# An attention-and-mixer kernel on one core: attention's work items given new spacings, the turned queries scaled in two instructions, and more filler matmuls in the first batch

## The chip, the core and the metric

The kernel runs on one core of one Trainium2 chip. The metric is device time in microseconds (us), lower is better. A single execution was also taken by the hardware profiler; the trace comes from that execution. The engines are named as in the profile: PE (TensorE, matmuls; PEld are its weight loads), DVE (VectorE), ACT (ScalarE), POOL (GpSimd) and SP (SyncE, which here only issues DMAs; SPq is its queue). L402 is line 402 of the kernel before.

## The reference, cut to what matters

```
q, k, v: 8 batches x 12 heads x 448 tokens x 64        (float32)
q_n = q / sqrt(mean(q*q) + 1e-6) * g_q                  (k_n likewise with g_k)
attn = softmax(q_n @ k_n^T / 8) @ v                     per head
x = attn as 8 x 448 x 768                               heads side by side
u = x + ((x^T @ U) @ V)^T                               rank 32, over the tokens
out = u + relu(u @ w_ch1) @ w_ch2                       768 -> 3072 -> 768
```

So each of the 8 batches has an attention part (12 heads) and a mixer part (the rank-32 step and the two large matmuls). The two large matmuls are most of PE's work.

## The kernel before, in words

**Units.** Heads are handled in pairs, six pairs to a batch; two pairs (four heads) form a group, so there are 24 groups, 0 to 23, three to a batch. A group's q, k and v are loaded together by `load`.

**Preparing a group.** `squares` (L138 on ACT or L140 on POOL) squares q and k, `sums` (L159, DVE) adds up each token's squares, `roots` (L165 and L166, ACT) makes the reciprocal root, and `scale` or `scale_dma` (POOL: L169, or L188 and L192) multiplies q and k with it, giving `qn` and `kp`. `values` (L196, L198) casts v. `scale_all` is roots, both scalings and values. Then q and k must be turned so that the 64 features lie on partitions. Groups 0 to 5 (batches 0 and 1) are turned by PE: `turn` (L343, seven transposes of 128 columns), followed by copies on DVE (`take_q` L352, which also multiplies by the gain `gg`; `take_k` L358 and L361). Groups 6 to 23 are turned by DMA: `turn_dma` issues four DMA transposes on SP, in the order q of the first pair (L367), k of the first pair (L369), q of the second, k of the second. Then `take_dma` multiplies the turned q by the gain, on POOL (L374), in one instruction over both pairs. It writes in place, so the scores of either pair read its result.

**Attention of a pair (b, pr).** The scores lie with keys on partitions, in four row blocks r = 0 to 3. `Sc` (L402) is the matmul of one block; r = 0, 1, 2 are two matmuls of 64 rows each (one for each head, on the two halves of the array), r = 3 is one matmul of 128 rows for the last 64 keys of both heads. The exponential of the block follows on ACT (L403) and writes `E`. The score tiles of r < 3 take turns in two PSUM buffers (`ps_sc`); all other PSUM tiles share four (`ps`). `V` (L420, L424) is one half of attn @ v, for 256 queries. It needs the exponentials of all four blocks. Its result is divided by the row sums on DVE (L427, L428) into x.

**The mixer of a batch.** `mix_t` and `mix_tr` (L441, L448) are the rank-32 step's first half, `mix_rows` (L490, L493) its second; DVE adds x (L498), and the sum is turned by a DMA transpose on SP (L502) into `uT`. In batch 0 `mix`, `mix_t0` and `up_part` do the same with PE. `up(b, ht)` (L508) is one of 24 blocks of the first large matmul, six matmuls of 448 columns; relu on ACT (L510). `down` (L534) is a quarter of one output tile of the second large matmul, six matmuls of 384 columns; DVE adds u (L542) and SP stores (L550).

**What sets the order.** All engines run their own queue in the order in which the program emits instructions. The emission is one list on the attention side (`att`) and one on the mixer side (`mlp`). Each item has a cost, given by hand. After the first batch's attention, the loop at L765 takes the next attention item as soon as the attention cost so far (`ca`) is not above `due(cm)`, the share that corresponds to the mixer cost emitted so far (`cm`), and otherwise a mixer item. So a larger cost on an attention item means that more of the mixer is emitted *behind* it before the next attention item. Items of cost 0 (loads, scalings, sums) follow at once. Attention runs ahead of the mixer by 1.8 batches (`LEAD`).

**The order on the attention side** for batches 1 to 7 is written in the loop at L613. For the first pair of a group (a = 0): the scores r = 0 and 1; V of the pair before, both halves; then three score blocks in one item (r = 2 of this pair, r = 0 of the next pair, r = 3 of this pair), so three exponentials come in a row; the group after is scaled (`scale_all`) or turned (`turn_dma`, `take_dma`); the first half of V. For the second pair (a = 1): r = 1, 2, 3 in one item; for groups up to 5 the two turns `T`; the second half of V of the pair before.

**The first batch** has no mixer work to put beside attention. Its items are listed in `extra` (L578), with `keep_busy(n)` (L232) after some score blocks: n matmuls of 128 columns of the identity by itself, which nobody reads.

Of the kernel before, what the change touches and what calls it, by code (L numbers as in the profile page):

```python
# [13 lines left out]
ALU = AluOpType  # L14
# [10 lines left out]
def kernel(  # L25
# [13 lines left out]
    nc = tc.nc  # L39
# [213 lines left out]
    gg = consts.tile([P, 2], FP32)  # L253
# [117 lines left out]

    def take_dma(gi):
        qT = q_bufs[gi % 2]
        nc.gpsimd.tensor_scalar(qT, qT, gg[:, 0:1], None, ALU.mult)  # L374
        for a in range(2):
            qk[(gi, a)] = [qT[:, a], kT_bufs[gi % 2][:, a]]

    def T(gi, i):
        if gi >= DMA_FROM:
            if i == 0:  # L380
                take_dma(gi)
            return
        turn(gi, i)
        for a in range(2):
            (take_q, take_k)[i](gi, a)
# [167 lines left out]
    pairs = [(b, pr) for b in range(B) for pr in range(NPAIR)]  # L553
    att = []

    def add_att(cost, f, *a):
        att.append((cost, f, a))
# [9 lines left out]
    def V2(i, half):  # L567
        return (0.55, V, (*pairs[i], half))
# [3 lines left out]
    def scales(gi):  # L572
        return [(0, roots, (gi,)), (0, scale, (gi, 0, pool)), (0, scale, (gi, 1, pool))]

    def turns(gi):
        return [(0.4, turn, (gi, 0)), (0, take_q, (gi, 0)), (0, take_q, (gi, 1)), (0.4, turn, (gi, 1)), (0, take_k, (gi, 0))]
# [3 lines left out]
        (0, 1): [(0, keep_busy, (8,))],  # L580
        (0, 2): scales(1) + [(0, squares, (2, 1, pool)), (0, keep_busy, (8,))],
        (0, 3): [(0, keep_busy, (8,))],
        (1, 1): [V2(0, 0)],
        (1, 2): [(0.4, turn, (1, 0)), (0, take_q, (1, 0)), (0, take_q, (1, 1))],
        (1, 3): [(0.4, turn, (1, 1)), (0, take_k, (1, 0)), V2(0, 1), (0, take_k, (1, 1)), (0, sums, (2, 1)),
                 (0, values, (1,)), (0, load, (4,)), (0, weights, (1,))],
        (2, 1): scales(2) + [(0, weights, (1,)), V2(1, 0)],
        (2, 3): [V2(1, 1), (0, prep_u, ())],
        (3, 1): [V2(2, 0)],
        (3, 2): turns(2),  # L590
        (3, 3): [V2(2, 1), (0, take_k, (2, 1)), (0, squares, (3, 0, pool)), (0, values, (2,)), (0, load, (5,)),
# [21 lines left out]
    for i, (b, pr) in enumerate(pairs):  # L613
        if b == 0:
            continue
        gi, a = divmod(i, 2)
        more = gi + 1 < len(groups)
        by_dma = gi + 1 >= DMA_FROM
        soon = gi + 2 < len(groups)

        nxt = pairs[i + 1 - a]

        if pr == 0 and b > 1:
            add_att(0.55, V, *pairs[i - 1], 0)
            add_att(0.55, V, *pairs[i - 1], 1)
        if a == 0:
            add_att(0.5, Srows, ((b, pr, 0), (b, pr, 1)))
            if i == 2 * DMA_FROM - 2:
                add_att(0.0, load, DMA_FROM + 1)
            if by_dma and more:  # L630
                add_att(0.0, scale_all, gi + 1)
            if b == 1 and pr == 0:
                add_att(0.4, lambda: None)
            if not by_dma:
                add_att(0.0, squares, gi + 1, 0, nc.gpsimd)
                add_att(0.0, squares, gi + 1, 1, nc.gpsimd)
                if gi + 2 >= DMA_FROM:
                    add_att(0.0, load, gi + 2)
            if pr != 0:
                add_att(0.55, V, *pairs[i - 1], 0)  # L640
                add_att(0.55, V, *pairs[i - 1], 1)
            add_att(0.7, Srows, ((b, pr, 2), (*nxt, 0), (b, pr, 3)))
            if not by_dma:
                add_att(0.0, sums, gi + 1, 0)
                add_att(0.0, sums, gi + 1, 1)
            if more and by_dma:
                add_att(0.0, turn_dma, gi + 1)
                add_att(0.0, take_dma, gi + 1)
                if gi + 1 == DMA_FROM:
                    add_att(0.0, weights, 2)  # L650
                if gi + 3 < len(groups):
                    add_att(0.0, load, gi + 3)
            if not by_dma:
                add_att(0.0, scale_all, gi + 1)
            add_att(0.55, V, b, pr, 0)
        else:
            add_att(0.7, Srows, ((b, pr, 1), (b, pr, 2), (b, pr, 3)))
            if more and not by_dma:
                add_att(0.39, T, gi + 1, 0)
            if soon and gi + 2 >= DMA_FROM:  # L660
                add_att(0.0, squares, gi + 2, 0)
                add_att(0.0, squares, gi + 2, 1)
            add_att(0.55, V, *pairs[i - 1], 1)
            if more and not by_dma:
                add_att(0.39, T, gi + 1, 1)
            if soon and gi + 2 >= DMA_FROM:
                add_att(0.0, sums, gi + 2, 0)
                add_att(0.0, sums, gi + 2, 1)
# [96 lines left out]
    while ia < len(att) or im < len(mlp):  # L765
# [6 lines left out]
        if take_att:  # L772
            c, f, a = att[ia]
# [11 lines left out]
        else:  # L785
            c, f, a, _ = mlp[im]
# [34 lines left out]
```

## Time and profile before

| what | us |
|---|---|
| median of three timed runs (597.79 to 599.4) | 598.76 |
| the profiled execution's own time | 596.07 |
| its span in the profile | 594.3 |
| PE busy in it | 574.3 |
| ACT busy | 307.4 |
| POOL busy | 201.9 |
| DVE busy | 196.5 |

The profiled execution's own time is 1.8 us more than its span, which begins and ends with the first and last recorded instruction. In the profile's timeline a row gives the start of the first and the length until the modelled end of the last of a run of like instructions, and in brackets how long the engine had been idle before and what ended that. Matmuls overlap: a run of six `up` matmuls has a length of 1.30 us, but the next instruction starts 1.13 to 1.14 us after it. So an idle time in brackets is a little shorter than the time by which the next matmul was late.

### The profile page before, as it was taken

What the parts mean: (1) busy time and instruction counts of PE and PEld (TensorE: products, weight loads), DVE (VectorE), ACT (ScalarE), POOL (GpSimd) and SP (SyncE); (2) the same over time, 40 slices, a digit from 0 to 9 for tenths busy, and PEclk for the clock granted to TensorE, in tenths of its full rate; (3) what the DMA queues carried; (4) which work ended last, traced back from release to release, by engine and by line L of the source; (5) the groups of instructions that cost most, each with busy time, mean ns of one, the idle gap of its engine ahead of it and who ended that gap; (6) DMA issues with size and microseconds to landing.
All of it is one profiled execution on the core that took longest, in us unless ns stands there. A gap on an engine that the chain in (4) does not pass through costs nothing.

```text
span 594.3 us, 11608 instructions
## 1 busy us (share of the span) xinstructions
PE 574.3 (97%) x4792; PEld 333.5 (56%) x4792; DVE 196.5 (33%) x454; ACT 307.4 (52%) x482; POOL 201.9 (34%) x288
## 2 busy tenths in 40 slices
PE   8799998999999999999999999999999999999996
PEld 7554455555566555655566555565556655655563
DVE  6775544512334312621235320541234310410011
ACT  7767784467453775466753568346753254014200
POOL 6995565243153333515053514424243000000000
PEclk9899999999999999999999999999999999999999
DMA  9999999573346550693164742566015210220022
GB/s 233 200 241 239 257 193 195 118 191 72 101 90 173 146 127 16 120 238 100 36 150 99 180 106 34 147 152 175 2 34 112 50 28 0 60 68 1 0 55 53
DMA packets 104508, 68.19 MB, mean 115 GB/s; under 512 B 66568, under 2 KB 101256, under 8 KB 104456
## 3 DMA queue, kind: packets, MB, share of 16 engines
q1 hardware_dynamic: 95044, 58.03, 41.0%
q0 software_dynamic: 9408, 9.44, 9.6%
q8 instruction: 37, 0.61, 0.4%
q14 instruction: 15, 0.12, 0.1%
q10 hardware_dynamic: 4, 0.00, 0.0%
HBM read 52.20 MB, written 11.01 MB: 106 GB/s over the span
## 4 chain that ended last, share of the span: by engine, by line
PE 90%; DMA 3%; ACT 3%; POOL 1%; DVE 1%; SPq 1%; issue 1%; POOLq 0%; ACTq 0%
PE ph L508 36%; PE po L534 36%; PE pv L424 6%; PE sc L402 5%; ACT E L403 2%; PE sl L402 2%; PE pv L420 2%; PE pm L493 2%; DMA qT<-qn 1%; DMA vf<-in_v_dram 1%; POOL qT L374 1%; PE pt L343 1%; PE pu L441 1%; DVE ssq L159 1%; ACT hT L510 0%
## 5 line engine op out<-in xcount | busy, mean ns | idle before, releaser
L534 PE MATMUL po<-w2b,hT 128*128 128x384 bf16 x1344 | 238.0, 326 | 0.0
L508 PE MATMUL ph<-uT,w1b 128*128 128x448 bf16 x1140 | 229.4, 352 | 0.0
L403 ACT ACTIVATE E<-sc,gg 128x896 bf16<-128x896 f32 (+1 forms) x150 | 140.3, 990 | 120.6 <-PE sc L402 120.4
L534 PEld LDWEIGHTS <-hT 128*128 128x128 bf16 x1344 | 126.0, 98 | 77.3 <-issue 3.7
L510 ACT ACTIVATE hT<-ph 128x448 bf16<-128x448 f32 x190 | 102.1, 548 | 119.7 <-PE ph L508 118.7
L508 PEld LDWEIGHTS <-w1b 128*128 128x128 bf16 x1140 | 108.0, 98 | 95.2 <-issue 3.0
L188 POOL TENSOR_TENSOR qn<-qf,rs 128x384 bf16<-128x384 f32 x36 | 29.9, 829 | 140.5 <-ACT rs L166 137.4
L427 DVE RECIPROCAL r<-pv 128x4 f32<-128x4 f32 x96 | 17.5, 182 | 178.9 <-PE pv L424 178.5
L374 POOL TENSOR_SCALAR qT<-qT,gg 128x896 bf16<-128x896 bf16 x18 | 45.4, 2522 | 90.1 <-DMA qT<-qn 68.9
L542 DVE TENSOR_TENSOR ob<-po,x 128x384 f32<-128x384 f32 x48 | 26.7, 557 | 115.4 <-PE po L534 115.4
L424 PE MATMUL pv<-va,E 128*128 128x65 bf16 x1152 | 57.6, 194 | 0.0
L424 PEld LDWEIGHTS <-E 128*128 128x128 bf16 x1152 | 51.0, 98 | 6.3 <-issue 0.2
L402 PE MATMUL sc<-qT,kT 64*128 64x448 bf16 (+1 forms) x294 | 43.9, 356 | 7.9 <-ACT E L403 3.8
L159 DVE TENSOR_REDUCE ssq<-sq 128x14 f32<-128x896 f32 x45 | 46.7, 1077 | 3.2 <-ACT sq L138 3.1
L420 PE MATMUL pv<-vl,E 128*128 128x130 bf16 x192 | 42.4, 221 | 2.8 <-ACT E L403 2.7
L428 DVE TENSOR_TENSOR x<-pv,r 128x256 bf16<-128x256 f32 x96 | 40.8, 425 | 3.3
L402 PEld LDWEIGHTS <-kT 64*128 64x128 bf16 (+1 forms) x336 | 14.1, 94 | 46.1 <-issue 42.6
L498 DVE TENSOR_TENSOR x<-pm,x 128x384 bf16<-128x384 f32 x48 | 26.5, 554 | 23.4 <-PE pm L493 19.3
L188 POOL TENSOR_TENSOR kp<-kf,rs 128x384 bf16<-128x384 f32 x36 | 29.8, 828 | 0.0
L403 ACT ACTIVATE E<-sl,gg 128x448 bf16<-128x448 f32 x42 | 26.9, 639 | 0.0
L420 PEld LDWEIGHTS <-E 128*128 128x128 bf16 x192 | 18.8, 98 | 13.1 <-ACT E L403 5.0
L196 POOL CAST va<-vf 128x768 bf16<-128x768 f32 x24 | 20.6, 860 | 0.0
(92 smaller groups left out, 299.7 us busy)
## 6 DMA issues: line engine op xcount, KB each, us to landing
qf<-in_q_dram SPq DMA_DIRECT2D x23, 448.0 KB, 3.6
kf<-in_k_dram SPq DMA_DIRECT2D x23, 448.0 KB, 5.6
out_dram<-ob SPq DMA_DIRECT2D x50, 192.0 KB, 2.7
vf<-in_v_dram SPq DMA_DIRECT2D x48, 192.0 KB, 5.9
w1b<-in_moe_w_ch_dram POOLq DMA_DIRECT2D x4, 1152.0 KB, 18.2
w2b<-in_moe_w_ch_dram POOLq DMA_DIRECT2D x8, 576.0 KB, 14.0
vf<-in_v_dram SPq DMA_DIRECT2D x48, 32.0 KB, 4.9
out_dram<-ob SPq DMA_DIRECT2D x12, 96.0 KB, 3.4
```

The source lines that it names most:

```text
L159: nc.vector.tensor_reduce(ssqs[gi][:, i, :], sqs.pop((gi, i)), AX, ALU.add)
L188: nc.gpsimd.tensor_tensor(main.rearrange("p (t i) d -> p i t d", i=2), src[:, c, :2 * NJ].rearrange("p (i t) d -> p i t d", i=2), rs[:, c, ...
L374: nc.gpsimd.tensor_scalar(qT, qT, gg[:, 0:1], None, ALU.mult)
L402: nc.tensor.matmul(sc[:, i, :S], kT[d, keys], qT[d], start=True, stop=True)
L403: nc.scalar.activation(es[(b, pr)][:, 2 * r:2 * r + n, :], sc[:, :n, :S], AF.Exp, scale=scal, bias=bias)
L420: nc.tensor.matmul(pv[:, i].rearrange("p e d -> p (e d)"), E[:, 2 * NJ, w:w + P], vl[:, lp, :], start=True, stop=False)
L424: nc.tensor.matmul(pv[:, i, e, :], E[:, 2 * j + e, w:w + P], va[:, (first_h + step * e) * NJ + j, :], start=False, stop=(e == 1 and j == N ...
L428: nc.vector.tensor_tensor(xs[b].rearrange("p i (h d) -> p i h d", d=D)[:, 2 * half:2 * half + 2, h0:h0 + step + 1:step, :], pv[:, :, :, :D ...
L508: nc.tensor.matmul(ph, w1b[:, dt, ht * P:(ht + 1) * P], uT[:, dt, off:off + S], start=(dt == 0), stop=(dt == KD - 1))
L510: nc.scalar.activation(hT[:, ht, off:off + S], ph, AF.Relu)
L534: nc.tensor.matmul(po, hT[:, ht, col:col + P], w2b[:, ht, half * HALF:(half + 1) * HALF], start=(ht == 0), stop=(ht == KH - 1))
L542: nc.vector.tensor_tensor(ob[:, h], po, urows(b, col, half), ALU.add)
```

## The change

Three things are changed.

1. `take_dma` scales the turned q pair by pair: two POOL instructions of 448 columns in place of one of 896.
2. Five `keep_busy` items are added to the first batch: 8 matmuls after the scores (1, 0), 6 after V in (1, 1), 8 after the turn in (1, 2), 6 after (2, 2) and 6 after (3, 0); with the existing fillers of 8 in (0, 0) to (0, 3) there are nine.
3. The costs in the loop are changed: 0.5 to 0.45 for the pair of score blocks, 0.7 to 1.0 for the three score blocks of a first pair, 0.7 to 0.6 for those of a second pair, 0.55 to 0.4 or 0.5 for the halves of V, 0.4 to 0.8 for an empty item at the start of batch 1. Both turns `T` of a group now follow each other on the list, ahead of the second half of V. The rest of the list is in the same order as before: the V items of a batch's first pair are only written at another place, and `(b, pr + 1, 0)` is what `(*nxt, 0)` was.

```diff
     def take_dma(gi):
         qT = q_bufs[gi % 2]
-        nc.gpsimd.tensor_scalar(qT, qT, gg[:, 0:1], None, ALU.mult)
         for a in range(2):
+            nc.gpsimd.tensor_scalar(qT[:, a], qT[:, a], gg[:, 0:1], None, ALU.mult)
             qk[(gi, a)] = [qT[:, a], kT_bufs[gi % 2][:, a]]
...
-        (1, 1): [V2(0, 0)],
-        (1, 2): [(0.4, turn, (1, 0)), (0, take_q, (1, 0)), (0, take_q, (1, 1))],
+        (1, 0): [(0, keep_busy, (8,))],
+        (1, 1): [V2(0, 0), (0, keep_busy, (6,))],
+        (1, 2): [(0.4, turn, (1, 0)), (0, take_q, (1, 0)), (0, take_q, (1, 1)), (0, keep_busy, (8,))],
...
+        (2, 2): [(0, keep_busy, (6,))],
         (2, 3): [V2(1, 1), (0, prep_u, ())],
+        (3, 0): [(0, keep_busy, (6,))],
...
-        if pr == 0 and b > 1:
-            add_att(0.55, V, *pairs[i - 1], 0)
-            add_att(0.55, V, *pairs[i - 1], 1)
         if a == 0:
-            add_att(0.5, Srows, ((b, pr, 0), (b, pr, 1)))
+            if pr == 0 and b > 1:
+                add_att(0.5, V, *pairs[i - 1], 0)
+                add_att(0.5, V, *pairs[i - 1], 1)
+            add_att(0.45, Srows, ((b, pr, 0), (b, pr, 1)))
...
             if b == 1 and pr == 0:
-                add_att(0.4, lambda: None)
+                add_att(0.8, lambda: None)
...
             if pr != 0:
-                add_att(0.55, V, *pairs[i - 1], 0)
-                add_att(0.55, V, *pairs[i - 1], 1)
-            add_att(0.7, Srows, ((b, pr, 2), (*nxt, 0), (b, pr, 3)))
+                add_att(0.4, V, *pairs[i - 1], 0)
+                add_att(0.5, V, *pairs[i - 1], 1)
+            add_att(1.0, Srows, ((b, pr, 2), (b, pr + 1, 0), (b, pr, 3)))
...
-            add_att(0.55, V, b, pr, 0)
+            add_att(0.4, V, b, pr, 0)
         else:
-            add_att(0.7, Srows, ((b, pr, 1), (b, pr, 2), (b, pr, 3)))
+            add_att(0.6, Srows, ((b, pr, 1), (b, pr, 2), (b, pr, 3)))
             if more and not by_dma:
                 add_att(0.39, T, gi + 1, 0)
+                add_att(0.39, T, gi + 1, 1)
...
-            add_att(0.55, V, *pairs[i - 1], 1)
-            if more and not by_dma:
-                add_att(0.39, T, gi + 1, 1)
+            add_att(0.5, V, *pairs[i - 1], 1)
```

More of the change, by code (lines that the diff above doesn't have):

```diff
@@ L619 @@
         soon = gi + 2 < len(groups)
-        nxt = pairs[i + 1 - a]
-        if pr == 0 and b > 1:
-            add_att(0.55, V, *pairs[i - 1], 0)
-            add_att(0.55, V, *pairs[i - 1], 1)
         if a == 0:
-            add_att(0.5, Srows, ((b, pr, 0), (b, pr, 1)))
+            if pr == 0 and b > 1:
+                add_att(0.5, V, *pairs[i - 1], 0)
+                add_att(0.5, V, *pairs[i - 1], 1)
+            add_att(0.45, Srows, ((b, pr, 0), (b, pr, 1)))
             if i == 2 * DMA_FROM - 2:
```

## The prediction

> **What bounds the kernel now.** I read the page first, then a table of stretches, then PE's timeline where it idles.
>
> ```profile
> span 594.3 us, 11608 instructions
> ...
> PE 574.3 (97%) x4792; PEld 333.5 (56%) x4792; DVE 196.5 (33%) x454; ACT 307.4 (52%) x482; POOL 201.9 (34%) x288
> ```
>
> PE works 97% of the span, so a change can only gain what PE idles (20.0 us) or what PE does more slowly than it could. The table says where the idle lies (columns: stretch, length, busy of each engine, granted clock, DMA share, GB/s).
>
> ```profile
> 0.00:45.00 45.00, 37.49 (x460) 27.34 (x461) 31.96 (x89) 32.44 (x50) 37.10 (x53) 0.96 0.98 224
> 45.00:120.00 75.00, 68.20 (x625) 38.95 (x623) 36.02 (x86) 45.70 (x71) 39.43 (x49) 1.00 1.02 203
> 120.00:370.00 250.00, 250.00 (x2072) 141.13 (x2069) 76.74 (x167) 148.65 (x233) 90.79 (x139) 1.00 0.49 115
> 370.00:380.00 10.00, 9.27 (x105) 5.90 (x104) 5.20 (x11) 4.73 (x8) 5.61 (x7) 1.00 0.59 151
> ```
>
> Before 45 us PE idles 7.51 us, from 45 to 120 (batch 1's attention and its mixer neighbours) 6.80, near 375 once 0.73, and nowhere else until the last 5.0 of the 20.0, at the end. So from 120 us on new spacings can only lose; the prize lies before. PE's timeline names every gap of the first of these:
>
> ```profile
> 50.28 0.36 PE L402 MATMUL sc<-qT,kT 64*128 64x448 bf16 x2 [0.41 <-ACT E L403]
> ...
> 50.77 0.33 PE L490 MATMUL pm<-x,Vm 128*128 128x384 bf16 x1
> 50.94 1.30 PE L508 MATMUL ph<-uT,w1b 128*128 128x448 bf16 x6
> 53.03 0.23 PE L420 MATMUL pv<-vl,E 128*128 128x130 bf16 x1 [0.80 <-ACT E L403]
> ...
> 61.06 0.55 PE L402 MATMUL sc<-qT,kT 64*128 64x448 bf16 x4 [0.45 <-DVE kT L358]
> ...
> 66.21 0.55 PE L402 MATMUL sc<-qT,kT 64*128 64x448 bf16 x4
> 66.69 0.36 PE L402 MATMUL sl<-qT,kT 128*128 128x448 bf16 x1
> 66.89 0.33 PE L490 MATMUL pm<-x,Vm 128*128 128x384 bf16 x1
> 67.05 1.30 PE L508 MATMUL ph<-uT,w1b 128*128 128x448 bf16 x6
> 69.23 0.23 PE L420 MATMUL pv<-vl,E 128*128 128x130 bf16 x1 [0.88 <-ACT E L403]
> ...
> 76.41 0.55 PE L402 MATMUL sc<-qT,kT 64*128 64x448 bf16 x4
> ...
> 84.41 0.23 PE L420 MATMUL pv<-vl,E 128*128 128x130 bf16 x1 [1.04 <-ACT E L403]
> ...
> 84.91 1.14 PE L534 MATMUL po<-w2b,hT 128*128 128x384 bf16 x6
> 85.98 0.55 PE L402 MATMUL sc<-qT,kT 64*128 64x448 bf16 x4
> ...
> 91.07 1.14 PE L534 MATMUL po<-w2b,hT 128*128 128x384 bf16 x6
> 94.01 0.56 PE L402 MATMUL sc<-qT,kT 64*128 64x448 bf16 x4 [1.80 <-POOL qT L374]
> ...
> 114.33 0.56 PE L402 MATMUL sc<-qT,kT 64*128 64x448 bf16 x4 [1.42 <-POOL qT L374]
> ```
>
> The seven idles add up to 6.80, the whole of it. A late matmul costs a little more than its idle: the six matmuls at 67.05 are followed after 1.14 when nothing waits, so V at 69.23 could have begun at 68.19 and is 1.04 late. In the same way the seven are late by 0.57, 0.96, 0.51, 1.04, 1.20, 1.87 and 1.50, together 7.65 us.
>
> Two kinds matter. V, at 53.03, 69.23 and 84.41, is emitted too close behind three exponentials; scores, at 94.01 and 114.33, wait for the scaling of the turned q.
>
> **Part 1: spacing behind the three exponentials.** From the first of the three score blocks at 66.21 to V at 69.23 are 3.02 us: that is the time which ACT needs. PE's work between them is blocks 0.68, `mix_rows` 0.16, one `up` 1.14: 1.98. I lay out the changed order with these prices, and with V 0.49 (84.41 to 84.91), `down` 0.97 and 0.10 to enter 64-row scores (84.91 to 85.98 together):
>
> - V of (1, 2): two `up` now lie between, 3.12. The wait of 1.04 goes.
> - V of (1, 4): `up` and `down`, 2.79. 1.20 becomes 0.23.
> - V of (1, 0): still `up` and `mix_rows`, 1.98, so 1.04 remains. But its second score block no longer waits for a score buffer, since two `up` and a `mix_rows` now precede it: 0.57 + 0.96 becomes 1.04.
> - Scores at 61.06: V and an `up` now lie between the turn and them. 0.51 goes.
> - Batches 2 to 7: the shortest such distance was 2.96 and becomes 4.27. PE has no idle there today, so nothing is gained.
>
> What is late next? The turns of groups 4 and 5 on PE, which follow sooner, while their preparation hangs on the same exponentials:
>
> ```profile
> 66.75 1.90 ACT L403 ACTIVATE E<-sc,gg 128x896 bf16<-128x896 f32 x2
> ...
> 69.96 0.32 ACT L165 ACTIVATE rs<-ssq,eps 128x28 f32<-128x28 f32 x1 [0.35 <-DVE ssq L159]
> ```
>
> ```profile
> 54.37 1.69 POOL L169 TENSOR_TENSOR qn<-qf,rs 128x896 bf16<-128x896 f32 x1 [6.24 <-DVE x L428]
> ...
> 70.61 1.69 POOL L169 TENSOR_TENSOR qn<-qf,rs 128x896 bf16<-128x896 f32 x1 [6.53 <-ACT rs L166]
> 72.26 1.69 POOL L169 TENSOR_TENSOR kp<-kf,rs 128x896 bf16<-128x896 f32 x1
> ```
>
> From `mix_rows` (whose DVE addition stands ahead of the sums) to a finished qn are 5.29 us in group 4 (50.77 to 56.06) and 5.41 in group 5 (66.89 to 72.30); roots, scaling and turn queue behind one another. Changed order, counted from the first of the three blocks: in group 4 `mix_rows` comes at 1.82, so qn is ready at about 7.15, while PE reaches the turn at 3.02 + 0.49 + 1.14 + 0.10 + 0.68 + 1.14 = 6.57: a new wait of 0.60. In group 5 `mix_rows` comes at 0.68, and one more relu stands ahead of the roots: qn at 6.2 against PE at 5.53, a new wait of 0.72; then the turn of k, at 7.78 against 7.89, 0.11.
>
> Balance of this part: 0.57 + 0.96 + 0.51 + 1.04 + 1.20 = 4.28 before, 1.04 + 0.60 + 0.72 + 0.11 + 0.23 = 2.70 after, **gain 1.6**.
>
> **Part 2: q scaled per pair.**
>
> ```profile
> 82.13 1.32 SPq L367 DMA_TRANSPOSE qT<-qn  x1
> 84.20 1.20 SPq L369 DMA_TRANSPOSE kT<-kp  x1
> 85.50 1.20 SPq L367 DMA_TRANSPOSE qT<-qn  x1
> ```
>
> ```profile
> 85.47 1.71 POOL L281 DMA_DIRECT2D w2b<-in_moe_w_ch_dram  x2
> 91.43 2.52 POOL L374 TENSOR_SCALAR qT<-qT,gg 128x896 bf16<-128x896 bf16 x1 [4.25 <-DMA qT<-qn]
> ```
>
> ```profile
> 85.50 5.73 DMA qT<-qn
> ```
>
> The one scaling waits for the *second* pair's q (issued 85.50, landed 91.23) though the scores at 94.01 need the first pair's, issued 3.4 us earlier. In the changed program each half waits for its own transpose. Price of a half: between 1.26 (half of 2.52) and 2.52 (all fixed cost); POOL's scaling of 896 columns takes 1.69 (L169) and of 384 columns 0.82, so nearly proportional, and I take 1.26. For the first q's landing no row stands alone: its issue plus 5.73 is 87.86. POOL is free at 87.18, so q is ready at 87.86 + 0.20 + 1.26 = 89.3, 12.9 us after the scores (1, 4, 0), which began at 76.41; k of the same pair is issued earlier than the second q and lands between. The scores wanted both at 92.14. But the order takes 1.1 us of PE work out of that distance, and the wait at 84.41 shrinks: PE asks 13.6 us after (1, 4, 0). Slack 0.7, so **1.87 goes**. With a half at 2.52 a wait of 0.6 would stay. The second pair's scores come 6.4 us later; with the same 5.73 its k (issued 1.25 after q) is there 3.8 us before.
>
> Group 7 (114.33): the first pair's q is issued two transposes (2.5 us) before the second's and its half takes 1.26 less, so it is ready 3.8 earlier. Against that, PE work between `turn_dma` and the scores falls by 1.1 (9.5 to 8.4), and one more x transpose stands ahead on SP, at most 1.3: 1.4 remain, and I count **the 1.50 as gone.** Groups 8 to 23 lose up to 2.3 us of distance and gain the 3.8; today none of them waits.
>
> **Part 3: the fillers.** Thirty-four matmuls.
>
> ```profile
> 11.30 0.62 PE L235 MATMUL busy<-ident 128*128 128x128 bf16 x8
> ```
>
> Eight last 0.62, the modelled tail included, so 34 cost at most 34/8 of it, 2.6 us, if on the path. Their cover is the waiting of PE in the first batch, for ACT and POOL:
>
> ```profile
> PE sc L402 <- ACT E L403: 3.4, 7, 0.9
> ...
> PE pt L343 <- POOL kp L169: 0.9, 1, 0.9
> ```
>
> Each new filler stands ahead of one of these waits or of the turn that waits for POOL, and holds PE for at most 0.62; I cost them at 0 (range 0 to 0.8 if the score behind a filler reaches ACT late). What they may bring is the clock:
>
> ```profile
> 21.69:25.10 3.41, 1.87 (x29) 1.27 (x29) 2.81 (x7) 3.12 (x6) 2.98 (x3) 1.00 0.49 84
> 25.10:28.51 3.41, 3.41 (x37) 2.71 (x34) 3.21 (x8) 2.50 (x4) 3.39 (x3) 0.50 1.11 213
> ```
>
> A stretch with PE busy for 1.87 of 3.41 is followed by one at half clock. The fillers after (2, 2) and (3, 0) put 0.67 into the first. At full clock the second would take PE up to 1.7 less, but DVE is behind it:
>
> ```profile
> 27.97 0.38 DVE L361 COPY kT<-pt 64x64 bf16<-64x64 bf16 x2
> ```
>
> That is the end of kT for the next scores, 28.35; they began 0.36 later, at 28.71. DVE's queue ahead of it (sums, casts, copies) does not depend on PE's clock. So 0.3 is gained, from 0 (the stretch stays slow) to 1.7. The Trainium skill's page "TensorE: Matmul & The Clock Gate", in "Why this matters for your kernels", asks for "No PE-idle gaps >~3µs between matmul bursts" against a fall to half clock. By that rule the fillers would change nothing, as no idle here is that long, and 0.3 would fall out of the sum, which would be 5.0 and 593.8; but this trace does show half clock behind idles of at most 0.89 us, so the row decides.
>
> **Sum.** 1.6 + 1.87 + 1.50 + 0.3 = 5.3 us off the profiled execution's own 596.07 (span 594.3 and 1.8 around it): 590.8. The median of the timed runs is 598.76, 2.7 above the profiled one; I carry the gain over unchanged: **593.5**.
>
> **Rivals.**
>
> 1. *Half the gain.* The first q or k of group 6 lands late, because DMA is full there and PE now asks 2 us sooner, or the halves cost 2.52: the wait of 1.87 stays, and some waits like those at the turns come on top. Gain 1.8 to 3.2, 595.6 to 597.0. For it: slack of only 0.7. Chance 0.16.
> 2. *More.* The new waits at the turns (1.43) don't form, the clock gives 1.7 in place of 0.3, and the wait of 1.04 at (1, 0) shrinks by some tenths: 7 to 8.5, 590.3 to 591.8. Chance 0.08.
> 3. *No change*, within 0.3% (1.8 us, about what a measurement of this kernel can tell from no change): the fillers are on the path (2.6) and rival 1 holds as well. About 598. Chance 0.13.
> 4. *Slower.* Place: the transposes of group 6, in the stretch with the fullest DMA. Mechanism: the first scores of batch 2 hang on q's landing, and each us beyond the slack of 0.7 is a us lost. To end slower by 1.8 they must wait 5.3 + 1.8 = 7.1, so q must land 7.8 later than reckoned, 13.5 us after its issue where 5.73 is the longest seen. 600.6 or more. Chance 0.08.
>
> That each half still waited for both transposes would be rival 1.
>
> **How the numbers follow.** Forecast (gain 3.2 to 7): 0.55. Range 590.3 to 597.5: the upper end is gain 1.3, with the group 6 wait kept, 1 us more there, no clock gain and 0.8 for fillers (5.3 - 1.87 - 1.0 - 0.3 - 0.8 = 1.3), the lower end the gain of 8.5 of rival 2. Faster by over 0.3%: 0.55 + 0.16 + 0.08 = 0.79; within: 0.13; slower: 0.08.
>
> **What the changed profile would show.** Right: PE idle in the stretch of batch 1 (45 to 120) near 3 us in place of 6.80; no wait of scores for L374's successor; V of (1, 2) without a wait; new waits of the turns (L343) for POOL's L169 of 0.4 to 0.7; clock 1.00 up to 45 us; nothing new after 120, and the 0.73 near 375 unchanged, as the order around it is. Wrong: idle after 120 us; scores waiting for a DMA of kT or qT; the fillers followed by ACT idle.

## The result, and the profile after

The changed kernel is faster: 593.59 us against 598.48 (medians of four runs each, 592.51 to 594.95 and 597.79 to 599.4), ratio 0.9918, 95% interval 0.9892 to 0.9944. In the experiments both kernels were timed again beside each other, with more runs: 592.18 against 596.93, ratio 0.9914 (0.9897 to 0.9931). So the timed gain is 4.8 to 4.9 us by the medians.

The two profiled executions differ by much less: 596.07 before, 594.04 after, 2.0 us. That gap between two profiles and two medians is the first thing to explain.

The page's head of the changed kernel, as quoted of before:

```profile
span 592.3 us, 11701 instructions
...
PE 575.5 (97%) x4826; PEld 334.2 (56%) x4826; DVE 195.5 (33%) x454; ACT 306.7 (52%) x482; POOL 206.6 (35%) x306
```

The table of stretches, with the same columns (stretch, length, busy of each engine, granted clock, DMA share, GB/s):

```profile
0.00:45.00 45.00, 37.86 (x486) 27.66 (x487) 31.11 (x89) 31.91 (x49) 34.92 (x50) 1.00 1.00 223
45.00:120.00 75.00, 71.11 (x655) 40.41 (x654) 36.89 (x89) 45.76 (x71) 43.10 (x58) 1.00 1.01 203
120.00:370.00 250.00, 250.00 (x2073) 141.37 (x2072) 76.00 (x166) 149.72 (x235) 95.34 (x148) 1.00 0.52 117
370.00:380.00 10.00, 9.26 (x107) 5.86 (x105) 6.50 (x14) 3.48 (x6) 5.04 (x10) 1.00 0.44 125
```

Between 45 and 120 us PE now idles 3.89 in place of 6.80; nothing new after 120; the 0.74 near 375 is as before; the clock is full up to 45. PE's timeline names what is left. These rows answer to the seven waits shown of before:

```profile
35.61 0.35 PE L466 MATMUL ph<-Vm,x 128*128 128x448 bf16 x1 [1.08 <-POOL Vm L314]
...
54.44 0.23 PE L420 MATMUL pv<-vl,E 128*128 128x130 bf16 x1 [0.88 <-ACT E L403]
...
58.57 0.56 PE L343 MATMUL pt<-ident,qn 128*128 128x128 bf16 x7 [0.42 <-POOL qn L169]
59.55 1.30 PE L508 MATMUL ph<-uT,w1b 128*128 128x448 bf16 x6 [0.25 <-ACT E L403]
...
72.95 0.56 PE L343 MATMUL pt<-ident,qn 128*128 128x128 bf16 x7 [0.47 <-ACT E L403]
...
91.48 0.55 PE L402 MATMUL sc<-qT,kT 64*128 64x448 bf16 x4
...
103.89 0.22 PE L420 MATMUL pv<-vl,E 128*128 128x130 bf16 x1 [0.82 <-DVE ob L542]
...
112.26 0.55 PE L402 MATMUL sc<-qT,kT 64*128 64x448 bf16 x4
118.79 2.44 PE L508 MATMUL ph<-uT,w1b 128*128 128x448 bf16 x12 [0.98 <-DMA uT<-u_rest]
```

The scores at 91.48 and 112.26 wait for nothing: these two waits are gone. The waits at 54, 58 and 73 us were forecast. Four were not: for `Vm` at 35 us, a PSUM buffer at 59, an output buffer whose store has not landed at 103, and the transposed last rows of the mixer (`u_rest`) at 118. POOL's rows show the halves (start, length):

```profile
88.69 1.41 POOL L375 TENSOR_SCALAR qT<-qT,gg 128x448 bf16<-128x448 bf16 x1
92.95 1.41 POOL L375 TENSOR_SCALAR qT<-qT,gg 128x448 bf16<-128x448 bf16 x1 [2.85 <-DMA qT<-qn]
109.45 1.41 POOL L375 TENSOR_SCALAR qT<-qT,gg 128x448 bf16<-128x448 bf16 x1 [8.83 <-DMA qT<-qn]
```

The first half of group 6 is done at 90.10, before the second q has landed and 1.38 ahead of the scores.

### The profile page after: what moved, and what is told of

It reads as the page before. It is cut to its first block, busy times and chain, and to the rows that moved or that the text cites. A ratio compares the mean times of both kernels' runs of the same rounds, so it can differ in the third digit from the quotient of the medians.

```text
span 592.3 us, 11701 instructions
## 1 busy us (share of the span) xinstructions
PE 575.5 (97%) x4826; PEld 334.2 (56%) x4826; DVE 195.5 (33%) x454; ACT 306.7 (52%) x482; POOL 206.6 (35%) x306
## 4 chain that ended last, share of the span: by engine, by line
PE 81%; DMA 12%; POOL 3%; issue 1%; DVE 1%; SPq 0%; ACT 0%; POOLq 0%; DVEq 0%
PE po L534 34%; PE ph L508 32%; PE pv L424 5%; PE sc L402 4%; DMA vf<-in_v_dram 4%; DMA qf<-in_q_dram 3%; DMA kf<-in_k_dram 2%; PE sl L402 2%; PE pm L493 2%; PE pv L420 1%; DMA kT<-kp 1%; DMA out_dram<-ob 1%; DMA uT<-u_rest 1%; POOL kp L169 1%; PE pu L441 0%
## 5 line engine op out<-in xcount | busy, mean ns | idle before, releaser
L375 POOL TENSOR_SCALAR qT<-qT,gg 128x448 bf16<-128x448 bf16 x36 | 50.6, 1405 | 72.0 <-DMA qT<-qn 62.5
L542 DVE TENSOR_TENSOR ob<-po,u_rest 128x384 f32<-128x384 f32 x8 | 4.5, 558 | 47.2 <-PE po L534 47.2
```

Source lines behind the costliest of these rows:

```text
L375: nc.gpsimd.tensor_scalar(qT[:, a], qT[:, a], gg[:, 0:1], None, ALU.mult)
L542: nc.vector.tensor_tensor(ob[:, h], po, urows(b, col, half), ALU.add)
```

## The experiments

The kernels of one series ran on one chip beside runs of before, so ratios are to that series' before: 597.51 (25 runs, 595.83 to 600.56), 596.93 (17 runs), 597.28 (19 runs). The ratios are not quotients of the medians and differ from these by up to 0.0013. "Late" is, as in the prediction, how much later a matmul begins than the one ahead of it allows; but from here on the 0.10 that the prediction allows for entering 64-row scores is not taken off, so scores read 0.10 higher (the 0.51 at 61 us is 0.62 here).

### First series: each part alone, and before once more

**Before, unchanged.**

> The kernel before, unchanged, profiled a second time, because the two profiled executions differ by only 2.0 us (596.07 and 594.04) while the medians of the timed runs differ by 4.9. Theory (the waits of the first 120 us are the same in every execution, and the first profiled execution of before was a lucky one by some 2.7 us of DMA arrival or clock in the first 45 us): this profiled execution has an own time of 597 to 599, PE idles 6.5 to 7.2 between 45 and 120 us as before, and the surplus stands ahead of 45 us. Rival (the profile makes no difference between executions, and the gain lies in something that the profiled execution does not show): own time 596 again, with the same idle in every stretch.

597.69, ratio 0.9997 (0.9979 to 1.0015). The profiled execution was 595.93, span 594.2, so again at the low end of the runs (595.93 to 598.6), with the same waits and an idle of 7.00 between 45 and 120 us. The theory's own sign (a dearer profile) did not come; the rival's did. But the runs show what is behind the gap: both profiled executions of before were of its cheapest, and the medians of this series lie 1.6 to 1.8 us above this one.

```profile
45.00:120.00 75.00, 68.00 (x624) 38.84 (x622) 35.66 (x86) 45.52 (x70) 39.23 (x50) 1.00 1.02 203
```

**The fillers alone.**

```diff
+        (1, 0): [(0, keep_busy, (8,))],
+        (1, 1): [V2(0, 0), (0, keep_busy, (6,))],
...
```

> The kernel before with the five new entries of fillers and nothing else (34 small matmuls in the first batch). Theory (the fillers are covered by PE's waiting in the first batch and bring only a fraction of a dip of the clock): 0.3 us faster, from 0.8 slower to 1.5 faster, 597.2 to 599.5. Rival (what the timed runs gain beyond the two profiles, 4.9 - 2.0 = 2.9 us, is a clock that dips in most executions of before and that the fillers hold up): at least 2.5 us faster, 596.0 or less, with granted clock 1.00 in all slices of the first 45 us.

596.43, ratio 0.9993 (0.9975 to 1.0011): no gain that can be told from none, and surely not 2.5. The first rival falls. The trace holds something else, in stretches of 3.41 us around the scores that wait for the scaling of q:

```profile
91.21:94.62 3.41, 0.82 (x7) 0.29 (x5) 1.53 (x6) 0.00 (x0) 2.52 (x1) 0.98 1.39 145
94.62:98.03 3.41, 3.41 (x14) 1.50 (x12) 0.00 (x0) 2.34 (x4) 0.84 (x2) 0.52 1.15 297
```

In this execution the second q landed later, the scores were 2.75 late, PE worked 0.82 of one stretch, and the next stretch ran at half clock (0.52 in the row). A long wait can be paid twice.

**The halves of q alone.**

```diff
-        nc.gpsimd.tensor_scalar(qT, qT, gg[:, 0:1], None, ALU.mult)
         for a in range(2):
+            nc.gpsimd.tensor_scalar(qT[:, a], qT[:, a], gg[:, 0:1], None, ALU.mult)
```

> The kernel before with the turned q scaled in two halves and nothing else. Theory (the two waits of scores for the one scaling, 1.87 at 94 us and 1.50 at 114 us, both go): 3.4 us faster, about 595.1, with no wait of scores for L373's successor and nothing new. First rival (what stands behind these waits is late as well: the output buffer's store, 0.98 us, and the last transpose of the mixer's rows, 1.14 us, which are the new waits of the changed kernel): only 3.4 - 2.1 = 1.3 us faster, 597.2, with these two waits in the trace. Second rival (the halves cost 1.41 each and the slack was too small): 1.5 faster, with a wait of about 1.8 left at the first scores of batch 2.

592.62, ratio 0.993 (0.9905 to 0.9955), about 4.2 us by the ratio (the whole change, below: 5.1) and 4.9 by the medians (4.8). Neither rival holds. In the trace the two waits are gone, none takes their place, and the span is 590.6, 3.6 less than that of before in this series, whose two waits were 1.92 and 1.83, together 3.75 (3.55 with the 0.10 taken off). The table's row for the stretch, and the first `up` of batch 1:

```profile
45.00:120.00 75.00, 71.41 (x654) 40.43 (x653) 36.61 (x89) 46.63 (x73) 42.27 (x57) 1.00 1.05 208
```

```profile
116.97 2.43 PE L508 MATMUL ph<-uT,w1b 128*128 128x448 bf16 x12
```

It keeps all five waits of batch 1's spacing (0.58, 0.97, 0.62, 1.04, 1.21) and idles 3.59 here, between the 3.89 and the 3.16 of the changed kernel's two profiles.

**The spacing alone.**

```diff
-            add_att(0.7, Srows, ((b, pr, 2), (*nxt, 0), (b, pr, 3)))
+            add_att(1.0, Srows, ((b, pr, 2), (b, pr + 1, 0), (b, pr, 3)))
...
```

> The kernel before with the new spacings and order of attention's items and nothing else: q is still scaled in one piece, no new fillers. Theory (the parts hang together: what the spacing takes out ahead of the first scores of batch 2 is given back there, as these still wait for the second q's transpose and one scaling of 2.52): 4.28 becomes 2.70 ahead of these scores, but the wait of 1.87 grows by the 1.1 us of PE work that goes out of the distance and by the 0.97 of the shrunken wait, and that of 1.50 by 1.1 to 2.4, so 1.6 to 2.9 us SLOWER than before, about 600.1 to 601.4, with waits of scores for the scaling of 3 to 4 us at about 92 us and of 2.6 to 3.9 us at about 115 us. Rival (the parts are independent and add up): 1.6 us faster, 596.9, with these two waits unchanged.

601.04, ratio 1.0053 (1.0032 to 1.0074): 3.2 us SLOWER by the ratio. The parts do not add up; the theory's sign holds and its size is a little short. The reason is in the waits (4.18 and 2.04 late) and behind each of them:

```profile
95.27 0.55 PE L402 MATMUL sc<-qT,kT 64*128 64x448 bf16 x4 [4.02 <-POOL qT L374]
...
118.71 0.56 PE L402 MATMUL sc<-qT,kT 64*128 64x448 bf16 x4 [1.88 <-POOL qT L374]
```

```profile
89.29:92.71 3.42, 1.96 (x24) 1.27 (x22) 3.18 (x7) 0.26 (x1) 0.01 (x1) 1.00 1.23 176
92.71:96.12 3.41, 0.85 (x6) 0.32 (x6) 0.00 (x0) 0.39 (x1) 2.51 (x1) 0.99 1.62 132
96.12:99.53 3.41, 3.41 (x12) 1.61 (x11) 0.00 (x0) 1.95 (x4) 1.34 (x3) 0.51 1.07 285
...
116.60:120.01 3.41, 1.53 (x11) 0.71 (x10) 2.54 (x3) 0.84 (x1) 2.05 (x1) 0.99 0.58 130
120.01:123.42 3.41, 3.41 (x24) 2.05 (x22) 0.00 (x0) 1.50 (x4) 1.80 (x3) 0.51 0.78 211
```

The stretches with 0.85 and 1.53 of PE work are followed by half clock, that with 1.96 is not. A later group's scores waited too, 1.37 late at 336 us. So without the halves the shorter distances cost more than the spacing saves.

### Second series: leaving one part out, and the half clock

**The changed kernel, unchanged.**

> The changed kernel, unchanged, beside its parts on the same chip. Theory: about 593 (592.3 to 594.5), with the two new waits of the first profile again (V of (2, 0, 0) some 1.0 us for the output buffer, the first up of batch 1 some 1.1 us for the last transpose of the mixer's rows), as both come of the order, and without the 1.1 us of the mixer for Vm, if that was an accident of a DMA's arrival. Rival: the two waits are accidents too, and are gone or much smaller.

592.18, ratio 0.9914 (0.9897 to 0.9931). The profiled span is 590.5, 1.8 less than in the first profile. `Vm` did not come again. The two late waits are still there, in other shares: 1.23 for the output buffer, 0.17 for `u_rest`, where the first profile had 0.98 and 1.14.

```profile
45.00:120.00 75.00, 71.84 (x654) 40.34 (x653) 36.46 (x89) 46.24 (x73) 41.96 (x56) 1.00 1.04 208
```

```profile
103.07 0.22 PE L420 MATMUL pv<-vl,E 128*128 128x130 bf16 x1 [1.06 <-DVE ob L542]
...
116.99 2.44 PE L508 MATMUL ph<-uT,w1b 128*128 128x448 bf16 x12
```

**Without the fillers.**

```diff
-        (1, 0): [(0, keep_busy, (8,))],
-        (1, 1): [V2(0, 0), (0, keep_busy, (6,))],
+        (1, 1): [V2(0, 0)],
...
```

> The changed kernel without the 34 fillers: spacing and the halves of q together. Theory: 593.3 to 594 (the fillers are worth 0.3), granted clock at half in one stretch of 3.41 us near 25 us, and nothing else different from the changed kernel. Rival (the fillers carry the gain of the timed runs): 595.5 or more.

592.5, ratio 0.9919 (0.9902 to 0.9935), 0.3 above the changed kernel and inside its interval. The half clock that was expected near 25 us did not come in this execution, although the fillers were out.

**Without the spacing.** The lines of the spacing as in before, the rest as changed.

```diff
-            add_att(1.0, Srows, ((b, pr, 2), (b, pr + 1, 0), (b, pr, 3)))
+            add_att(0.7, Srows, ((b, pr, 2), (*nxt, 0), (b, pr, 3)))
...
```

> The changed kernel with the old spacing and order: only the halves of q and the fillers. Theory now (the halves bring the whole gain; the spacing takes 1.5 us of waits away in batch 1 and brings 0.98 + 1.14 = 2.1 behind it, for the output buffer and the last transpose of the mixer's rows): 592.0 to 592.6, so 0.3 to 1.0 FASTER than the changed kernel, with the waits of V of 0.97, 1.04 and 1.21 in batch 1 and none at 103 and 118 us. Rival (as in the prediction: the spacing is worth 1.6 beside the halves): 594.3 or more, 1 us or more slower than the changed kernel.

593.27, ratio 0.9934 (0.9916 to 0.9953): 1.1 above the changed kernel, not below it. The two intervals overlap, though the runs hardly do (592.62 to 594.47 against 591.8 to 592.74). The theory that the spacing costs more than it brings is not borne out, and its sign was wrong: the waits at 102 us (1.22, output buffer) and 118 us (0.54, `u_rest`) are here too, beside the five of batch 1. They are not made by the spacing.

**The spacing alone, with matmuls in the two waits.**

```diff
+            if b == 2 and pr in (0, 2):
+                add_att(0.0, keep_busy, 40 if pr == 0 else 20)
             add_att(0.45, Srows, ((b, pr, 0), (b, pr, 1)))
```

> The spacing alone (q in one scaling) with 40 and 20 small matmuls put in front of the two scores that wait for the scaling (batch 2, first and third pair): 3.3 us of matmuls more, whose results nobody reads. Theory (a wait of 2 us or more is paid twice: the stretch of 3.41 us that follows a stretch with PE busy for 1.5 or less runs at half clock and costs another 1.7; matmuls in the wait keep the clock): the scores begin when they did, no half clock behind them, and the time FALLS by 1.7 to 3.4, from 601.0 to 597.6 to 599.3. Rival (the half clock costs nothing that matters, as what follows waits for others): 601.0 or up to 3.3 more.

599.32, ratio 1.0036 (1.0021 to 1.0052), against 1.0053 for the spacing alone: some 1.0 us less with 60 matmuls more. That is just above the range expected, and the two intervals overlap, so the times alone do not settle it. The trace does:

```profile
92.22 2.41 PE L235 MATMUL busy<-ident 128*128 128x128 bf16 x40 [0.33 <-DVE x L428]
95.57 0.55 PE L402 MATMUL sc<-qT,kT 64*128 64x448 bf16 x4 [0.93 <-POOL qT L374]
...
115.28 1.28 PE L235 MATMUL busy<-ident 128*128 128x128 bf16 x20
116.49 0.55 PE L402 MATMUL sc<-qT,kT 64*128 64x448 bf16 x4
```

The scores at 95.57 begin as late as they did (95.27), no half clock follows, and the next such scores are reached 19.71 us later (115.28) in place of 21.40 (118.71 less the 2.04 by which they were late): 1.69 us, about half of a stretch of 3.41, as half clock would take. What spoils the sum is a later group, 2.64 late:

```profile
331.32 2.52 POOL L374 TENSOR_SCALAR qT<-qT,gg 128x896 bf16<-128x896 bf16 x1 [12.37 <-DMA qT<-qn]
```

### Third series: what is late next, and what the halves do

**Three output buffers.**

```diff
-    outp = ctx.enter_context(tc.tile_pool(name="outp", bufs=2))
+    outp = ctx.enter_context(tc.tile_pool(name="outp", bufs=3))
```

> The changed kernel with three output buffers in place of two. Theory (the wait near 102 us, 0.98, 1.23 and 1.73 us in three profiled executions, is for an output buffer whose store has not landed): it goes, 1.0 to 1.7 us faster than the changed kernel, 590.5 to 591.2 where that measured 592.2. Rival (what stands behind it is as late, the last transpose of the mixer's rows for the first up of batch 1, which waited 1.14, 0.17 and not at all): the time stays within 0.5 of the changed kernel's and the wait moves to 117 us.

592.35, ratio 0.9919 (0.9901 to 0.9936): no gain; the rival holds. The wait at 102 us is gone and the one behind it has grown to 1.51:

```profile
117.00 1.31 PE L508 MATMUL ph<-uT,w1b 128*128 128x448 bf16 x6 [1.35 <-DMA uT<-u_rest]
```

The start of this `up` is the same as without the third buffer (116.99). SP's queue shows where the transpose stands (start, length; x2 are two in a row):

```profile
105.50 1.22 SPq L367 DMA_TRANSPOSE qT<-qn  x1
106.80 1.22 SPq L369 DMA_TRANSPOSE kT<-kp  x1
108.12 1.22 SPq L367 DMA_TRANSPOSE qT<-qn  x1
109.39 1.26 SPq L369 DMA_TRANSPOSE kT<-kp  x1
110.74 1.25 SPq L502 DMA_TRANSPOSE uT<-x  x1
112.08 1.18 SPq L550 DMA_DIRECT2D out_dram<-ob  x2
113.35 2.43 SPq L502 DMA_TRANSPOSE uT<-u_rest  x1
```

From 105.50 to 115.78 SP issues with hardly a pause, each transpose taking 1.22 or more.

**The old spacing from batch 2 on**, batch 1 as changed (the V that end it keep their 0.5). The other lines of the loop follow before in the same way.

```diff
+        if b > 1:
...
+                add_att(0.7, Srows, ((b, pr, 2), (*nxt, 0), (b, pr, 3)))
...
+        else:
...
```

> The changed kernel with the old spacing and order from batch 2 on; batch 1 as changed. Theory (as in the prediction: from 120 us on PE does not idle, so the spacing of batches 2 to 7 gains nothing and batch 1 has all of it): the changed kernel's time within 0.5, 591.7 to 592.7. Rival (the later batches carry the 1.1 us by which the changed kernel beat the halves and fillers alone): 593.0 or more.

592.58, ratio 0.992 (0.9903 to 0.9937): within 0.5 of the changed kernel. From batch 2 on the spacing does nothing that can be measured, as the prediction said. In its trace the wait for the output buffer is 2.00, the largest of all, and the first `up` of batch 1 begins at 117.23.

**Before, with matmuls in its two waits.**

```diff
+            if b == 2 and pr in (0, 2):
+                add_att(0.0, keep_busy, 14)
             add_att(0.5, Srows, ((b, pr, 0), (b, pr, 1)))
```

> The kernel before with 14 small matmuls, 0.78 us of them, in front of each of the two scores that wait for the scaling at 94 and 114 us; their results are read by nobody. Theory (before has two kinds of executions, near 596.2 and near 598.2, and the second kind is one in which the wait of 1.9 us falls whole into one stretch of 3.41 us, so that PE is busy for 1.5 of it and the next stretch runs at half clock, 1.7 us more): the scores begin when they did, the dear kind goes, and the median falls by 0.5 to 1.3, to 595.9 to 596.5. Rival (the two kinds come from elsewhere): the median stays within 0.3 of before's on the same chip, with as many runs above 597.5.

597.4, ratio 1.0015 (0.9983 to 1.0046): no fall, runs from 595.73 to 603.46. In the trace the matmuls stand in the waits and the scores begin when they did (94.02; before, in the first series, 93.57), but 6 of 12 runs lie above 597.5, as 8 of 19 of before do. So the theory that half clock behind these two waits makes the dear runs of before falls.

**Before, transposes in the order q, q, k, k**, one scaling.

```diff
         for a in range(2):
             rows = slice(a * R, (a + 1) * R)
             nc.sync.dma_start_transpose(q_bufs[gi % 2][:, a].rearrange("p (j r) -> p j r", r=R),
                                         normed[gi][0][rows].rearrange("p j c d -> p (j c d)"))
+        for a in range(2):
+            rows = slice(a * R, (a + 1) * R)
             nc.sync.dma_start_transpose(kT_bufs[gi % 2][:, a].rearrange("p (g r) -> p g r", r=R),
```

> The kernel before with the transposes issued in the order q, q, k, k, not q, k, q, k, and still one scaling of both halves. Theory (the scores of the two waits hang on the second q's landing and on nothing else): the second q is issued 1.25 to 2.1 us sooner, the wait of 1.87 falls to 0.6 or less and that of 1.50 to 0.25, 2.4 to 3.1 us off and no half clock behind them: 593.3 to 594.5 by before's 597. Rival (the landing does not follow the issue, as the transposes queue in the DMA engines, or the first k is late instead): 1 us or less off.

593.92, ratio 0.9938 (0.9914 to 0.9961), 3.4 us under before's 597.28: as the theory had it. Both q are issued one behind the other from 81.58 (the second had begun at 85.50 in before), the whole scaling begins at 88.24, and the scores do not wait at 91.6 and are 0.37 late at 110.7. The scaling itself takes 2.52 as in before.

```profile
81.58 2.65 SPq L367 DMA_TRANSPOSE qT<-qn  x2
84.35 2.51 SPq L371 DMA_TRANSPOSE kT<-kp  x2
88.24 2.52 POOL L376 TENSOR_SCALAR qT<-qT,gg 128x896 bf16<-128x896 bf16 x1 [1.59 <-DMA qT<-qn]
```

So what cost before its 3.4 us was the second q's place in SP's queue, not the length of the scaling; the halves are one cure and the order is another. Its runs spread over 4.8 us, though, from 592.4 to 597.16, where those of the kernels with halves spread over 0.8 to 3.0 in a series.

## Why the prediction was right, and where its steps were not

The time forecast, 593.5, and the median of 593.59 agree; the steps of the working agree less well. The gain was 4.9 in place of 5.3, and the times come closer than that only because the median of before, with a fourth run, came out at 598.48 and not 598.76.

**What bounds the kernel: right.** All that was gained lies between 45 and 120 us. In the pair of profiles without accidents (before in the first series, the changed kernel in the second), idle there falls from 7.00 to 3.16, 3.84, and the spans by 3.7 (594.2 to 590.5).

**Halves: right.** Both waits went, in every one of the six kernels with halves. A half takes 1.41, not 1.26, so two take 2.82 in place of 2.52. PE asked 13.62 after the scores (1, 4, 0) (77.86 to 91.48; 13.6 forecast), the half was done after 12.24 (12.9 forecast). In the first profile it did not even wait for its q: its row names no wait for a DMA, and it began when POOL was free. For group 7 there were 1.40 left (109.45 + 1.41 to 112.26), where the working had set 1.4 us of gain against a wait of 1.50 and so left nothing. Part of that is the wait for the output buffer, which makes PE come later; with three buffers 0.48 were left (108.23 + 1.40 to 110.11). Alone the halves measure 4.2 (2.7 to 5.7) for the 3.4 of the sum.

**The waits of the spacing: right one by one, the gain not.** Forecast and seen late, in the first profile: V of (1, 0) 1.04 and 1.05; the turns of q 0.60 and 0.58, 0.72 and 0.63; V of (1, 4) 0.23 and 0.23; the turn of k 0.11 and 0.12 (at 74.60). One of 0.42 at 59 us, for a PSUM buffer, was missed. So 4.28 became 3.03 in place of 2.70: about 1.3 us gained in batch 1, for the 1.6 of the sum. (One sum of the working is rounded loosely: 1.82 + 5.29 is 7.11, not 7.15.) The step that failed is the question "what is late next?", which the prediction put only to the turns of groups 4 and 5, and answered after 120 us with PE's lack of idle. It did not put it to the stores and to SP's queue between 100 and 118 us. There the time goes again: halves alone reach the first `up` of batch 1 at 116.97 without waiting late; the changed kernel reaches it at 116.99 after 1.40 of new waits, without fillers at 117.17, with three buffers at 117.00. The third buffer shows that removing one of the two waits only feeds the other. Without the spacing (118.24) and in the first profile (118.79) it was later still, by the same two waits. That the floor near 117.0 is SP's run of issues is read from the trace and was not tried by itself. Nor is it the issues alone: the last transpose landed 2.4 us after its issue with the halves alone, 3.6 with three buffers, 4.0 without the spacing and 4.2 in the first profile, and the starts at 118.24 and 118.79 are such late landings (issued at 114.23 and 114.55). What the spacing is worth beside the halves is thus between nothing (those starts) and 1.1 us (the medians with and without it, whose intervals overlap). Without the halves it costs 3.2.

**Fillers: as small as said.** 0.3 was taken; 0.4 (without halves: 0.0007 of 597.5; 1.1 by the medians) and 0.3 (592.5 to 592.18) were measured, neither to be told from zero. That the row decides against the rule on idle gaps in the Trainium skill's page "TensorE: Matmul & The Clock Gate", section "Why this matters for your kernels", was right in one respect: half clock does follow idles far below 3 us (at most 0.89 in before). But the dip near 25 us comes and goes without the fillers too.

**Carrying the gain over unchanged: a step that failed, and by luck made up for the other.** 5.3 was worked out for one profiled execution, where 3.7 is what such an execution really gains. The medians moved 4.8, because before's runs reach 3 to 7 us above its cheapest in a series and those of the changed kernel 0.9 (six runs) to 2.4. The cheapest runs of the second series differ by 3.8 (595.64 and 591.8), like the profiles. So 1.6 too much for the spacing was in part made up by about 1.1 of spread that had not been reckoned with. Where the dear runs of before lose their time stays open. The kernels with one scaling of both q spread more (2.6 to 7.7 us, though over more runs), and in two of them a later group's scores were seen waiting for that scaling (1.37 and 2.64 late near 335 us); that the same happens in dear runs of before is possible, but none of these was profiled, and matmuls in the two early waits did not help.

**The rivals.** None held. The slower one needed q of group 6 to land 13.5 us after its issue; here the first half of the scaling began 5.15 after it (83.54 to 88.69).

## What to carry to other kernels

When one instruction waits for two transfers and its first reader needs only one, look at where the second transfer stands in its queue: splitting the instruction or reordering the queue brings the same. When waits are taken away, ask what is late next along the whole way to the next long stretch without idle, the queue that issues DMAs included; what is late there can swallow gains that were each worked out nearly right. And compare medians of many runs before reading a gain from two profiles, as one profiled execution may be the cheapest of its kind.

## What the runs showed of the hardware

- Half clock came in stretches of 3.41 us on a grid of 3.41 us. In the 14 traces all six of them that stood inside the work followed a stretch in which PE was busy for 1.87 us or less (0.82, 0.85, 1.53, 1.59, 1.62, 1.87); after every one with 1.93 or more the clock stayed full, and between 1.44 and 1.87 it went both ways (1.44, 1.59 and 1.85 were also seen followed by full clock). Single waits of 4.18, 2.75 and 2.04 were enough; one of 2.64, whose stretch had PE busy for the 1.44, was not. The Trainium skill's page "TensorE: Matmul & The Clock Gate", in "What's actually happening", has the gate watch a free-running window of 3413 ns; the traces agree on the length, and a grid that lies elsewhere in each execution would explain why the same wait is followed by half clock in one run and not in another.
- Such a stretch, with PE fully used, cost 1.69 us in the one place where it was read (21.40 against 19.71 for the same work).
- POOL's scaling of bf16 in place takes 1.41 us for 448 columns and 2.52 for 896, so about 0.30 of each would be fixed, an estimate from these two.
